# Attention and MLP on one core: weights converted without GpSimd, masks computed from indices, and the MLP's matmuls dealt out singly with a lag

## The chip, the cores and the metric

One core of a Trainium2 chip. The metric is the device time of one launch in microseconds (us), median of repeated runs. The program uses one core, so there is no second core to compare with. The experiments were made on three chips; on each, the kernel before was timed in the same rounds, with medians of 871.7 to 873.1 us.

## The reference, cut to what matters

```python
batch, n_heads, seq, head_dim = (4, 8, 768, 48)          # attention
n_tokens, d_model, d_ff = (3072, 384, 2048)              # MLP

for t in range(S):                                       # gated linear attention with a state
    state = f[:, :, t, :, None] * state + einsum('bhd,bhe->bhde', k[:, :, t], v[:, :, t])
    y[:, :, t] = einsum('bhd,bhde->bhe', q[:, :, t], state)
x = y.transpose(0, 2, 1, 3).reshape(B * S, H * D)        # the bridge
h = x @ w_in                                             # f = sigmoid(f_logit) above
g = h * sigmoid(1.702 * h)
out = g @ w_out
```

`w_in` and `w_out` reach the device as fp64; the kernel has to turn their bits into fp32 itself. Everything else is fp32.

## The kernel before

The attention is cut into 12 units of 256 positions. A unit is a list of parts. A "T" part is four TensorE transposes and a ScalarE copy out of PSUM; a "W" part is a level of scores, which TensorE computes, VectorE scales and masks, and TensorE applies to v. Two units make a pair, whose result xT (turned by DMA) feeds one MLP: 16 blocks "h" of three products of 512 columns, then 64 "o" products of 384 columns. (The trace records two matmuls for each of these products, hence 96 h and 128 o in its lines; "matmul" in the change is one product.) The TensorE order is fixed when the kernel is built, so work for the engine is put between the small dependent steps of the attention by emitting it there.

The conversion of one piece of weights uses three engines:

```python
WI, WO = 256, 192                                        # columns of a piece of w_in, w_out
def load_weights(n, dst, src):
    bits = wp.tile([P, w, 2], I32, tag="bits", bufs=4)
    nc.sync.dma_start(out=bits..., in_=src.bitcast(I32))
    lo, hi = bits[:, :, 0], bits[:, :, 1]
    nc.scalar.activation(sign, hi.bitcast(F32), AF.Sign)
    nc.scalar.activation(a, hi.bitcast(F32), AF.Abs, scale=2.0 ** 112)
    ve.tensor_scalar(a, a, 2.0 ** 97, None, op0=ALU.max)
    ve.tensor_scalar(s.bitcast(I32), a.bitcast(I32), 3, -(1 << 31), ...)      # shift, xor
    ve.tensor_scalar(a.bitcast(I32), s.bitcast(I32), -(1 << 23), None, op0=ALU.bitwise_and)
    ve.scalar_tensor_tensor(a, lo.bitcast(U32), 2.0 ** -52, a, op0=ALU.mult, op1=ALU.mult)
    po.tensor_tensor(a, a, s, ALU.add)                   # GpSimd
    po.tensor_tensor(dst, a, sign, ALU.mult)             # GpSimd
```

The MLP is a list of blocks, and `merge` emits blocks between the parts of a unit (cut):

```python
def mlp_h(g, s, xT, t0, t1):                             # one block: NK = 3 matmuls, sigmoid, product
    ...
    return [lambda ff=ff: block(ff) for ff in range(NFF)]
def mlp_o(g, s):                                         # one block: 4 matmuls
    ...
def merge(parts, fill, share):
    for i, (kind, fn) in enumerate(parts):
        fn()
        at += share(kind, i)
        while done < len(fill) * at / total:
            fill[done](); done += 1
...
for s in range(1, NALL // 2):                            # the schedule: the MLP of pair s in the next two units
    fill = mlp_h(g[s], s, xTs[s], 0, TM) + mlp_o(g[s], s)
    ...
    for j in range(2):
        merge(unit(2 * (s + 1) + j), fill[j * len(fill) // 2:(j + 1) * len(fill) // 2], even)
```

Nearly all DMAs are issued from SyncE's one queue: raw inputs, v, weights, xT and the output. The conversion of the weights is put in as fill too: pieces of `w_in` in unit 0, pieces of `w_out` in units 1 and 2.

## Time and profile before

| | kernel before |
|---|---|
| time, median of 3 runs | 871.22 us (870.77 to 872.17) |
| profiled span | 870.1 us |
| start of unit 1, 2, 3 (first transpose of each on TensorE) | 72.13, 159.94, 206.16 us |
| from the start of unit 3 to the end | 663.9 us |

The last two rows split the kernel into "the start", where the weights are still being converted, and "the rest". The prediction below shows the page and the waits. Here are busy times by stretch, each with the number of instructions. The first line of stretches is unit 0, the second roughly unit 1, the third one pair in the steady part. PEclk is the clock that TensorE was granted, as a share of full speed.

```profile
core 0: us, PE busy (x) PEld busy (x) DVE busy (x) ACT busy (x) POOL busy (x), PEclk, DMA share, GB/s
0.00:72.00 72.00, 29.24 (x592) 23.87 (x592) 50.28 (x105) 24.37 (x56) 41.17 (x65) 0.75 0.79 175
72.00:166.00 94.00, 57.81 (x721) 45.71 (x718) 68.49 (x180) 38.36 (x103) 52.61 (x78) 0.68 0.50 126
335.20:463.70 128.50, 119.57 (x1425) 69.90 (x1424) 43.50 (x61) 30.61 (x50) 6.29 (x12) 0.97 0.30 66
```

At the start no engine is full. In the steady pair TensorE lacks 8.9 us of being full, 6 of them in the one wait for xT that the prediction shows. The other part of those 8.9 us is in small waits, such as these two, where one block of transposes follows another with nothing put between (TensorE's timeline, start and duration; the bracket gives the idle time ahead and what ended it):

```profile
406.92 0.90 PE L199 MATMUL tf<-ident,raw 128*128 128x128 f32 x4
408.50 0.66 PE L199 MATMUL tq<-ident,raw 128*128 128x128 f32 x4 [0.69 <-ACT F L205]
...
411.58 0.60 PE L199 MATMUL tq<-ident,raw 128*128 128x128 f32 x4
412.90 0.66 PE L199 MATMUL tk<-ident,raw 128*128 128x128 f32 x4 [0.73 <-ACT X L207]
```

### The profile page before, as it was taken

Reading aid. Unit: us, or ns where it says so; the run is one execution under the profiler, and the core shown is the slowest. Engines: PE = TensorE matmul, PEld = TensorE weight load, DVE = VectorE, ACT = ScalarE, POOL = GpSimd, SP = SyncE. Lnnn points to the kernel's source line nnn. Section 1 sums busy time; section 2 is a strip of 40 time slices with the busy share of each in tenths; the row PEclk is TensorE's granted clock in tenths of the full one; section 3 lists DMA queues with packets and bytes.
Section 4 is the critical chain, followed back from the end, with each engine's and each line's share of the span. In section 5 each row is a group of like instructions: output and inputs, shape, how many; then the busy total and the mean of one; then the engine's idle time right before and its main releaser. Section 6 shows DMA issues by size and latency. Waiting matters only on the chain.

```text
span 870.1 us, 19829 instructions
## 1 busy us (share of the span) xinstructions
PE 745.9 (86%) x8672; PEld 460.9 (53%) x8672; DVE 345.8 (40%) x611; ACT 223.6 (26%) x429; POOL 126.3 (15%) x204
## 2 busy tenths in 40 slices
PE   2445367899996999996999996999997999989998
PEld 1343355677663555663555663555664555654454
DVE  3787778563330542321452321452322532312200
ACT  2334334433112323112223112223112232111200
POOL 7455555401001001001001001001001001000000
PEclk9855559799998999998999997999999999999999
DMA  9846624514514206223216123117134020000000
GB/s 211 176 117 178 138 75 141 119 27 116 78 58 99 38 11 141 43 73 83 37 29 133 33 85 79 30 39 131 25 90 84 2 84 28 11 26 12 0 19 18
DMA packets 132902, 63.41 MB, mean 73 GB/s; under 512 B 104144, under 2 KB 129744, under 8 KB 132816
## 3 DMA queue, kind: packets, MB, share of 16 engines
q1 hardware_dynamic: 132816, 62.15, 31.1%
q8 instruction: 68, 1.11, 0.6%
q14 instruction: 18, 0.15, 0.1%
HBM read 52.69 MB, written 9.44 MB: 71 GB/s over the span
## 4 chain that ended last, share of the span: by engine, by line
PE 71%; POOL 8%; issue 8%; ACT 4%; DMA 4%; SPq 4%; DVE 1%; POOLq 0%; ACTq 0%; DVEq 0%
PE h L412 28%; PE o L429 27%; PE sc L228 5%; PE y L277 4%; POOL a L140 4%; POOL w_out L141 2%; PE y L382 2%; SPq L394 2%; POOL w_in L141 2%; DMA vn<-v_tok 1%; DMA xT<-yT 1%; ACT X L207 1%; PE tq L199 1%; SPq L167 1%; PE tk L199 1%
## 5 line engine op out<-in xcount | busy, mean ns | idle before, releaser
L412 PE MATMUL h<-xT,w_in 128*128 128x512 f32 (+1 forms) x672 | 282.7, 569 | 31.0 <-DMA xT<-yT 25.7
L429 PE MATMUL o<-w_out,g 128*128 128x384 f32 x768 | 261.9, 491 | 0.0
L412 PEld LDWEIGHTS h<-xT,w_in 128*128 128x128 f32 x672 | 129.8, 202 | 142.1 <-issue 112.8
L429 PEld LDWEIGHTS o<-w_out,g 128*128 128x128 f32 x768 | 141.1, 190 | 90.4 <-issue 2.6
L418 DVE TENSOR_TENSOR g<-h,sg 128x512 f32<-128x512 f32 (+1 forms) x112 | 68.7, 614 | 243.3 <-ACT sg L417 243.3
L417 ACT ACTIVATE sg<-h 128x512 f32<-128x512 f32 (+1 forms) x112 | 59.8, 535 | 203.9 <-PE h L412 202.2
L264 DVE TENSOR_TENSOR X<-X,tot 128x1024 f32<-128x1024 f32 x60 | 73.2, 1220 | 89.9 <-PE sc L228 89.8
L214 POOL TENSOR_TENSOR tot<-F 128x512 f32<-128x512 f32 x12 | 12.7, 1055 | 530.1 <-ACT F L205 464.6
L228 PE MATMUL sc<-X,Kc 48*64 48x64 f32 x1920 | 45.6, 238 | 34.4 <-DVE A L248 34.1
L268 ACT COPY Kc<-X 128x512 f32<-128x512 f32 x60 | 37.7, 628 | 132.9 <-DVE X L264 132.9
L228 PEld LDWEIGHTS sc<-X,Kc 48*64 48x64 f32 x1920 | 37.8, 148 | 61.1 <-issue 27.4
L277 PE MATMUL y<-A,vl 64*48 64x64 f32 (+1 forms) x2688 | 65.4, 243 | 0.0
L248 DVE TENSOR_TENSOR A<-sc,masks 128x512 f32<-128x512 f32 (+1 forms) x84 | 62.9, 759 | 0.0
L277 PEld LDWEIGHTS y<-A,vl 64*48 64x48 f32 x2688 | 55.7, 132 | 2.3 <-issue 2.0
L140 POOL TENSOR_TENSOR a<-a,s 128x192 f32<-128x192 f32 (+1 forms) x56 | 41.1, 734 | 60.5 <-DVE a L139 58.9
L131 ACT ACTIVATE sign<-bits 128x192 f32<-128x192 f32 (+1 forms) x56 | 22.5, 401 | 73.0 <-POOL w_out L141 34.5
L435 ACT COPY osb<-o 128x384 f32<-128x384 f32 x24 | 11.5, 479 | 106.6 <-PE o L429 102.8
L388 ACT COPY yT<-y 48x1024 f32<-48x1024 f32 x24 | 24.2, 1006 | 47.7 <-PE y L382 47.4
L133 DVE TENSOR_SCALAR a<-a 128x192 f32<-128x192 f32 (+1 forms) x56 | 21.6, 387 | 37.1 <-ACT a L132 36.5
L228 PE MATMUL sc<-X 48*64 48x128 f32 (+1 forms) x768 | 27.2, 274 | 9.8 <-DVE A L248 9.1
L218 DVE TENSOR_TENSOR X<-X,F 128x512 f32<-128x512 f32 x24 | 21.3, 886 | 30.9 <-ACT X L207 30.9
L382 PE MATMUL y<-X,st 48*48 48x64 f32 x704 | 25.1, 228 | 9.0 <-DVE st L369 6.9
(38 smaller groups left out, 460.4 us busy)
## 6 DMA issues: line engine op xcount, KB each, us to landing
vl<-v_tok SPq DMA_DIRECT2D x84, 192.0 KB
bits<-in_moe_w_in_dram SPq DMA_DIRECT2D x24, 256.0 KB
bits<-in_moe_w_out_dram SPq DMA_DIRECT2D x32, 192.0 KB
raw<-in_f_logit_dram SPq DMA_DIRECT2D x24, 192.0 KB
raw<-in_q_dram SPq DMA_DIRECT2D x24, 192.0 KB
raw<-in_k_dram SPq DMA_DIRECT2D x24, 192.0 KB
v_tok<-in_v_dram SPq DMA_DIRECT2D x12, 384.0 KB
vn<-v_tok SPq DMA_DIRECT2D x12, 384.0 KB
```

Of the source, the lines that this page charges most:

```text
L140: po.tensor_tensor(a, a, s, ALU.add)
L141: po.tensor_tensor(dst, a, sign, ALU.mult)
L228: nc.tensor.matmul(out[g * HS:(g + 1) * HS, h, a, :], lhsT=lhs(h, a * U + g * G), rhs=rhs(h, a * U + g * G), start=True, stop=True,)
L248: nc.vector.tensor_tensor(A[:, :, c:c + w].rearrange("p h (x t) -> p h x t", t=64), t["sc"][:, :, c:c + w].rearrange("p h (x t) -> p h x t ...
L264: nc.vector.tensor_tensor(qk, qk, by, ALU.mult)
L268: nc.scalar.copy(Kc.rearrange("p (n m) -> p n m", m=m), X[:, 2].rearrange("p (n two m) -> p n two m", two=2, m=m)[:, :, 0, :],)
L277: nc.tensor.matmul(dst(h, g, a), lhsT=t["vl"][g * 64:(g + 1) * 64, u, (2 * a + h) * D:(2 * a + h + 1) * D], rhs=A(h, g, a), start=(start a ...
L382: nc.tensor.matmul(py[rows(h), c // 2, a, c % 2 * C:(c % 2 + 1) * C], lhsT=t["before"][c][rows(h), a], rhs=t["X"][rows(h), 1, x:x + C], st ...
L412: nc.tensor.matmul(ph[:, :T], lhsT=w_in[:, n, ff * P:(ff + 1) * P], rhs=xT[:, n, t0:t1], start=(n == 0), stop=(n == NK - 1),)
L417: nc.scalar.activation(sg[:, :T], ph[:, :T], AF.Sigmoid, scale=1.702)
L418: nc.vector.tensor_tensor(g[ff // FG][:, ff % FG, t0:t1], ph[:, :T], sg[:, :T], ALU.mult)
L429: nc.tensor.matmul(po, lhsT=g[ff // FG][:, ff % FG, tt * P:(tt + 1) * P], rhs=w_out[:, ff, :], start=(ff == 0), stop=(ff == NFF - 1),)
```

## The change

Five things at once. GpSimd and one ScalarE operation leave the conversion, which VectorE then does with six operations (ScalarE keeps one, the Abs); pieces of `w_out` are twice as wide (384 columns), and there are three landing buffers, in which the raw bits arrive, in place of four. The masks come from two index tiles and comparisons. The MLP lags: unit 3 gets 32 of its matmuls fewer, so that half an "o" product is still to do when a pair ends and xT is on its way. And the fill is dealt out matmul by matmul, by columns, where it went by blocks of three or four. At the start, four pieces are emitted ahead of everything, and the rest is spread differently over units 0 to 2.

The diff, cut (cuts marked with `...`):

```diff
-    full = mlp.tile([P, NL, G], F32, tag="g", name="full", bufs=5)
-    nc.gpsimd.memset(full, 1.0)
+    at = [wp.tile([P, 64], I32, tag="bits", name=f"at{j}", bufs=3) for j in range(2)]
+    nc.gpsimd.iota(at[0], ...); nc.gpsimd.iota(at[1], ...)
+    nc.vector.tensor_scalar(at[0], at[0], 63, None, op0=ALU.bitwise_and)
+    nc.vector.tensor_tensor(at[0], at[0], at[1], ALU.bitwise_xor)
     for l, m in enumerate(LEV):
-        ... two nc.gpsimd.affine_select per level, then one nc.gpsimd.tensor_tensor ...
+        nc.vector.tensor_scalar(masks[:, l, :], at[0], float(m), None, op0=ALU.is_lt)
...
-    WI, WO = 256, 192
+    WI, WO = 256, 384
...
-        bits = wp.tile([P, w, 2], I32, tag="bits", name=f"bits_{n}", bufs=4)
+        bits = wp.tile([P, w, 2], I32, tag="bits", name=f"bits_{n}", bufs=3)
...
-        nc.scalar.activation(sign, hi.bitcast(F32), AF.Sign)
         nc.scalar.activation(a, hi.bitcast(F32), AF.Abs, scale=2.0 ** 112)
+        ve.tensor_scalar(si, hi, -(1 << 31), -(1 << 31), op0=ALU.bitwise_and, op1=ALU.bitwise_xor)
         ve.tensor_scalar(a, a, 2.0 ** 97, None, op0=ALU.max)
-        ve.tensor_scalar(s.bitcast(I32), a.bitcast(I32), 3, -(1 << 31), ...)
-        ve.tensor_scalar(a.bitcast(I32), s.bitcast(I32), -(1 << 23), None, op0=ALU.bitwise_and)
+        ve.scalar_tensor_tensor(si, ai, 3, si, op0=ALU.logical_shift_left, op1=ALU.bitwise_xor)
+        ve.tensor_scalar(ai, si, -(1 << 23), None, op0=ALU.bitwise_and)
         ve.scalar_tensor_tensor(a, lo.bitcast(U32), 2.0 ** -52, a, op0=ALU.mult, op1=ALU.mult)
-        po.tensor_tensor(a, a, s, ALU.add)
-        po.tensor_tensor(dst, a, sign, ALU.mult)
+        ve.tensor_tensor(dst, a, s, ALU.add)
...
-        return [lambda ff=ff: block(ff) for ff in range(NFF)]
+        return [(T, lambda ff=ff, n=n: one(ff, n)) for ff in range(NFF) for n in range(NK)]
...
-            while done < len(fill) * at / total:
-                fill[done]()
-                done += 1
+            while fill and done < columns * at / total:
+                w, emit = fill.pop(0)
+                emit()
+                done += w
...
+    LAG = 32 * DM
...
+    for _ in range(4):
+        weights.pop(0)[1]()
+    ...
+    merge(unit(0), weights, W_IN - 4 * WI, windows)
+    first = unit(1)
+    merge(first[:8], weights, W_OUT // 6, steady)
+    fill = both(mlp_h(g[0], 0, 0, U), [weights.pop(0) for _ in range(len(weights) // 2)])
+    merge(first[8:], fill, NFF * NK * U, steady)
+    emit_all(fill)
+    fill = both(mlp_h(g[0], 0, U, TM), weights)
+    merge(unit(2), fill, NFF * NK * U, steady)
+    emit_all(fill)
+    fill = mlp_o(g[0], 0)
     for s in range(1, NALL // 2):
+        fill += mlp_h(g[s], s, 0, TM) + mlp_o(g[s], s)
+    for n in range(3, NALL):
+        merge(unit(n), fill, UNIT - (LAG if n == 3 else 0), steady)
+    emit_all(fill)
```

More of the change, by code (lines that the diff above doesn't have):

```diff
@@ L84 @@
     make_identity(nc, ident)
-    full = mlp.tile([P, NL, G], F32, tag="g", name="full", bufs=5)
-    nc.gpsimd.memset(full, 1.0)
-    for l, m in enumerate(LEV):
-        for base, step, chan in ((0, -m, 1), (m - 1, m, -1)):
-            nc.gpsimd.affine_select(
-                out=full[:, l, :], in_=full[:, l, :], compare_op=ALU.is_ge, fill=0.0, base=base,
-                pattern=[[step, G // m], [0, m]], channel_multiplier=chan,
-            )
-    masks = const.tile([P, NL, 64], F32, name="masks")
-    nc.gpsimd.tensor_tensor(masks, full[:, :, :64], full[:, :, 64:], ALU.add)
+    masks = const.tile([P, NL, 64], F32, name="masks")
+    at = [wp.tile([P, 64], I32, tag="bits", name=f"at{j}", bufs=3) for j in range(2)]
+    nc.gpsimd.iota(at[0], pattern=[[0, 64]], base=0, channel_multiplier=1)
+    nc.gpsimd.iota(at[1], pattern=[[1, 64]], base=0, channel_multiplier=0)
+    nc.vector.tensor_scalar(at[0], at[0], 63, None, op0=ALU.bitwise_and)
+    nc.vector.tensor_tensor(at[0], at[0], at[1], ALU.bitwise_xor)
+    for l, m in enumerate(LEV):
+        nc.vector.tensor_scalar(masks[:, l, :], at[0], float(m), None, op0=ALU.is_lt)
     raw = const.tile([P, 3, NG, H, HS], F32, name="raw")
@@ L118, in load_weights, with tmp @@
             return
-        bits = wp.tile([P, w, 2], I32, tag="bits", name=f"bits_{n}", bufs=4)
+        bits = wp.tile([P, w, 2], I32, tag="bits", name=f"bits_{n}", bufs=3)
         nc.sync.dma_start(out=bits.rearrange("p c two -> p (c two)"), in_=src.bitcast(I32))
         lo, hi = bits[:, :, 0], bits[:, :, 1]
-        def tmp(tag):
-            return wp.tile([P, w], F32, tag=tag, name=f"{tag}_{n}")
-        ve, po = nc.vector, nc.gpsimd
-        sign, a, s = tmp("sign"), tmp("a"), tmp("s")
-        nc.scalar.activation(sign, hi.bitcast(F32), AF.Sign)
+        def tmp(tag, bufs=2):
+            return wp.tile([P, w], F32, tag=tag, name=f"{tag}_{n}", bufs=bufs)
+        ve = nc.vector
+        a, s = tmp("a"), tmp("s")
+        ai, si = a.bitcast(I32), s.bitcast(I32)
         nc.scalar.activation(a, hi.bitcast(F32), AF.Abs, scale=2.0 ** 112)
+        ve.tensor_scalar(si, hi, -(1 << 31), -(1 << 31), op0=ALU.bitwise_and, op1=ALU.bitwise_xor)
         ve.tensor_scalar(a, a, 2.0 ** 97, None, op0=ALU.max)
-        ve.tensor_scalar(
-            s.bitcast(I32), a.bitcast(I32), 3, -(1 << 31), op0=ALU.logical_shift_left, op1=ALU.bitwise_xor
-        )
-        ve.tensor_scalar(a.bitcast(I32), s.bitcast(I32), -(1 << 23), None, op0=ALU.bitwise_and)
+        ve.scalar_tensor_tensor(si, ai, 3, si, op0=ALU.logical_shift_left, op1=ALU.bitwise_xor)
+        ve.tensor_scalar(ai, si, -(1 << 23), None, op0=ALU.bitwise_and)
         ve.scalar_tensor_tensor(a, lo.bitcast(U32), 2.0 ** -52, a, op0=ALU.mult, op1=ALU.mult)
-        po.tensor_tensor(a, a, s, ALU.add)
-        po.tensor_tensor(dst, a, sign, ALU.mult)
+        ve.tensor_tensor(dst, a, s, ALU.add)
     V_HALF = [(1, 0), (1, 1)] + [(m, 0) for m in LEV[1:]]
@@ L403, with mlp_h, one @@
     TM = 2 * U
-    def mlp_h(g, s, xT, t0, t1):
-        def block(ff):
-            if ff % FG == 0 and t0 == 0:
-                g.append(mlp.tile([P, FG, TM], F32, tag="g", name=f"g_{s}_{ff}", bufs=5))
-            T = t1 - t0
-            ph = ps.tile([P, TM], F32, tag="mm", name=f"h_{s}_{ff}_{t0}", bufs=3)
-            for n in range(NK):
-                nc.tensor.matmul(
-                    ph[:, :T], lhsT=w_in[:, n, ff * P:(ff + 1) * P], rhs=xT[:, n, t0:t1],
-                    start=(n == 0), stop=(n == NK - 1),
-                )
-            sg = mlp.tile([P, TM], F32, tag="sg", name=f"sg_{s}_{ff}_{t0}")
-            nc.scalar.activation(sg[:, :T], ph[:, :T], AF.Sigmoid, scale=1.702)
-            nc.vector.tensor_tensor(g[ff // FG][:, ff % FG, t0:t1], ph[:, :T], sg[:, :T], ALU.mult)
-        return [lambda ff=ff: block(ff) for ff in range(NFF)]
+    def mlp_h(g, s, t0, t1):
+        t = {}
+        T = t1 - t0
+        def one(ff, n):
+            if n == 0:
+                if ff % FG == 0 and t0 == 0:
+                    g.append(mlp.tile([P, FG, TM], F32, tag="g", name=f"g_{s}_{ff}", bufs=5))
+                t["ph"] = ps.tile([P, TM], F32, tag="mm", name=f"h_{s}_{ff}_{t0}", bufs=3)
+            ph = t["ph"]
+            nc.tensor.matmul(
+                ph[:, :T], lhsT=w_in[:, n, ff * P:(ff + 1) * P], rhs=xTs[s][:, n, t0:t1],
+                start=(n == 0), stop=(n == NK - 1),
+            )
+            if n == NK - 1:
+                sg = mlp.tile([P, TM], F32, tag="sg", name=f"sg_{s}_{ff}_{t0}")
+                nc.scalar.activation(sg[:, :T], ph[:, :T], AF.Sigmoid, scale=1.702)
+                nc.vector.tensor_tensor(g[ff // FG][:, ff % FG, t0:t1], ph[:, :T], sg[:, :T], ALU.mult)
+        return [(T, lambda ff=ff, n=n: one(ff, n)) for ff in range(NFF) for n in range(NK)]
@@ L421, in mlp_o, with one @@
     def mlp_o(g, s):
         t = {}
-        def some(tt, ff0):
-            if ff0 == 0:
+        def one(tt, ff):
+            if ff == 0:
                 t["po"] = ps.tile([P, DM], F32, tag="mm", name=f"o_{s}_{tt}", bufs=3)
             po = t["po"]
-            for ff in range(ff0, ff0 + 4):
-                nc.tensor.matmul(
-                    po, lhsT=g[ff // FG][:, ff % FG, tt * P:(tt + 1) * P], rhs=w_out[:, ff, :],
-                    start=(ff == 0), stop=(ff == NFF - 1),
-                )
-            if ff0 + 4 == NFF:
+            nc.tensor.matmul(
+                po, lhsT=g[ff // FG][:, ff % FG, tt * P:(tt + 1) * P], rhs=w_out[:, ff, :],
+                start=(ff == 0), stop=(ff == NFF - 1),
+            )
+            if ff == NFF - 1:
@@ L437, in some, with merge, steady, windows @@
                 nc.sync.dma_start(out=out[r0:r0 + P, :], in_=o)
-        return [lambda tt=tt, ff0=ff0: some(tt, ff0) for tt in range(TM // P) for ff0 in range(0, NFF, 4)]
-    def merge(parts, fill, share):
-        total = sum(share(kind, i) for i, (kind, _) in enumerate(parts))
+        return [(DM, lambda tt=tt, ff=ff: one(tt, ff)) for tt in range(TM // P) for ff in range(NFF)]
+    def merge(parts, fill, columns, share):
+        total = sum(share(kind) for kind, _ in parts)
         at = done = 0
-        for i, (kind, fn) in enumerate(parts):
+        for kind, fn in parts:
             fn()
-            at += share(kind, i)
-            while done < len(fill) * at / total:
-                fill[done]()
-                done += 1
-    def even(kind, i):
+            at += share(kind)
+            while fill and done < columns * at / total:
+                w, emit = fill.pop(0)
+                emit()
+                done += w
+    def steady(kind):
         return 3 if kind == "W" else 1
+    def windows(kind):
+        return kind == "W"
     xTs, loads = {}, {}
@@ L473, in load, with both, emit_all @@
         loads[n] = load_v(n)
-    weights = [lambda n=n, p=p: load_weights(n, *p) for n, p in enumerate(pieces_in + pieces_out)]
-    NI = len(pieces_in)
+    weights = [(p[0].shape[1], lambda n=n, p=p: load_weights(n, *p)) for n, p in enumerate(pieces_in + pieces_out)]
+    W_IN, W_OUT = NK * DFF, NFF * DM
+    UNIT = (NFF * NK * TM + TM // P * NFF * DM) // 2
+    LAG = 32 * DM
+    g = {s: [] for s in range(NALL // 2)}
+    def both(one, two):
+        a, b = sum(w for w, _ in one), sum(w for w, _ in two)
+        todo, out, at = list(two), [], 0
+        for w, emit in one:
+            out.append((w, emit))
+            at += w
+            while todo and b - sum(x for x, _ in todo) < b * at / a:
+                out.append((0, todo.pop(0)[1]))
+        return out
+    def emit_all(fill):
+        while fill:
+            fill.pop(0)[1]()
+    for _ in range(4):
+        weights.pop(0)[1]()
     load_raw(0)
     load(0)
-    merge(unit(0), weights[:NI], lambda kind, i: 1)
-    g = {s: [] for s in range(NALL // 2)}
-    u1 = unit(1)
-    merge(u1[:8], weights[NI:NI + 8], lambda kind, i: 1)
-    merge(u1[8:], weights[NI + 8:NI + 16] + mlp_h(g[0], 0, xTs[0], 0, U), lambda kind, i: 1)
-    merge(unit(2), [f for p in zip(mlp_h(g[0], 0, xTs[0], U, TM), weights[NI + 16:]) for f in p], even)
-    merge(unit(3), mlp_o(g[0], 0), even)
-    for s in range(1, NALL // 2):
-        fill = mlp_h(g[s], s, xTs[s], 0, TM) + mlp_o(g[s], s)
-        if s + 1 == NALL // 2:
-            for f in fill:
-                f()
-            continue
-        for j in range(2):
-            merge(unit(2 * (s + 1) + j), fill[j * len(fill) // 2:(j + 1) * len(fill) // 2], even)
+    merge(unit(0), weights, W_IN - 4 * WI, windows)
[8 more added lines that the diff above has]
+    fill = mlp_o(g[0], 0)
+    for s in range(1, NALL // 2):
+        fill += mlp_h(g[s], s, 0, TM) + mlp_o(g[s], s)
+    for n in range(3, NALL):
+        merge(unit(n), fill, UNIT - (LAG if n == 3 else 0), steady)
+    emit_all(fill)
 _INS = ['q', 'k', 'v', 'f_logit', 'moe_w_in', 'moe_w_out']
```

## The prediction

> **What bounds the kernel now.** I read the page first, then the chain of work that ended last, then the timeline of TensorE at the places where that chain leaves TensorE, then the waits of the stretch in which it lies on GpSimd. A "unit" below is the attention of 256 positions of one batch (12 of them); the MLP of a pair of units (the "h" product, then the "o" product) is put between the parts of later units.
>
> The page, part 2: two regimes. For about 165 us TensorE is half idle and at half clock while VectorE and GpSimd are busy (the fp64 weights are converted to fp32 there, 56 pieces); after 205 us TensorE is full with short dips, and the last 88 us are MLP alone.
>
> ```profile
> span 870.1 us, 19829 instructions
> PE   2445367899996999996999996999997999989998
> DVE  3787778563330542321452321452322532312200
> POOL 7455555401001001001001001001001001000000
> PEclk9855559799998999998999997999999999999999
> ```
>
> The chain of work, end of it: one MLP at full clock costs 42.25 + 41.29 = 83.5 us.
>
> ```profile
> 783.03 42.25 PE h L412 x94
> 825.28 41.29 PE o L429 x128
> ```
>
> The dips: TensorE's timeline where a pair of units ends. The last o of the old MLP and a transpose of the next unit are done, then h stands first in TensorE's fixed order and needs xT, which this pair's attention has only just produced and a DMA must turn. The waits of TensorE sum it up.
>
> ```profile
> 395.08 0.60 PE L199 MATMUL tf<-ident,raw 128*128 128x128 f32 x4
> 401.67 2.90 PE L412 MATMUL h<-xT,w_in 128*128 128x512 f32 x3 [5.99 <-DMA xT<-yT]
> ...
> 653.29 0.60 PE L199 MATMUL tf<-ident,raw 128*128 128x128 f32 x4
> 657.10 3.44 PE L412 MATMUL h<-xT,w_in 128*128 128x512 f32 x4 [3.21 <-issue]
> ```
>
> There are five: 7.0 us before 273.2, 6.0 before 401.7, 7.0 before 531.2, 3.2 before 657.1, 3.55 before 781.9, in sum 26.8 us. After each the clock is down: the chain shows the first six h at 5.11, 5.46, 5.46 and 4.32 us where six cost 2.59 later; excess 2.5 + 2.9 + 2.9 + 1.7 = 10.0 us.
>
> The start: in the waits between 83 and 166 us (unit 1) the longest are a ring: ScalarE waits for GpSimd to free the "sign" buffer, VectorE for ScalarE, GpSimd for VectorE; TensorE's scores wait behind it in VectorE's queue.
>
> ```profile
> POOL a L140 <- DVE a L139: 35.1, 28, 3.8
> ACT sign L131 <- POOL w_out L141: 34.5, 24, 3.4
> PE sc L228 <- DVE A L248: 23.5, 5, 6.5
> DVE a L133 <- ACT a L132: 15.3, 17, 2.9
> ```
>
> The reader is to see that no engine is saturated there: pieces go round at (89.3 - 17.0)/23 = 3.14 us for 256 columns and (171.4 - 90.0)/31 = 2.63 us for 192, by the first and last starts of the GpSimd multiplications, while one piece holds GpSimd for 1.2 to 1.5 us. The windows give unit 0 as 0 to 72 us, unit 1 as 72 to 166, unit 2 as 166 to 206.
>
> **What the Trainium skill says.** "GPSIMD Engine Reference", section Performance versus the Vector engine: two-input elementwise work is about half as fast there. The trace agrees: an addition of 128x256 takes 741 ns on GpSimd, VectorE's product of 128x256 420 ns. The same page, section Key points: it shares SBUF interfaces with VectorE, with contention when VectorE runs in a two-port mode. The trace agrees: the 256-wide TENSOR_SCALAR takes 0.29 us when GpSimd is idle (13.3 us), and 0.70 us at 15.9 us beside a GpSimd addition. "VectorE: DVE Perf Modes", section on the perf-mode tiers: fp32 tensor_scalar runs at 2x, tensor_tensor at 1x; here 0.29 against 0.42 us at 256 columns. "TensorE: Matmul & The Clock Gate", Part 1: the clock halves after an idle window of about 3.4 us and needs as much work to return; PEclk 0.50 between 40 and 80 us, and the slow h above, agree.
>
> **The change, part by part.**
>
> *Masks.* Fourteen GpSimd operations (8.2 us, until 9.5 us) become two iotas and eight VectorE operations of 64 columns. GpSimd's next work is at 14.5 us, so this was hidden: about 0.
>
> *Conversion.* Removed per piece: one ScalarE operation and two of GpSimd. VectorE goes from three TENSOR_SCALAR and one two-input operation to three and three. In the timeline independent TENSOR_SCALARs start 0.20 us apart (31.30, 31.51, 31.71) and a two-input one holds the engine 0.33 at 256 columns; at 192 it is 0.17 and 0.27. So 3 x 0.20 + 3 x 0.33 = 1.6 us, with some waits on the operation before 1.75 us for 256 columns; extended to 384 (0.26 and 0.45), 2.13, say 2.35 us. 24 x 1.75 + 16 x 2.35 = 80 us of VectorE. Attention costs VectorE per unit 6 x 1.14 + 1.14 + 6 x 0.60 + 2 x 0.60 + 7 x 0.39 = 15.5 us, the gating of half an h 16 x 0.33 = 5.3 us. So VectorE is what bounds units 0 and 1:
> - Unit 0: first weights land at 12.5 us as before, 19 pieces come ahead of its state update in VectorE's order: 12.9 + 19 x 1.75 + 15.5 = 62; with three landing buffers instead of four some waits on DMA: 68 us (was 72). Little gain, since VectorE takes over what GpSimd did.
> - Unit 1: 5 x 1.75 + 9 x 2.35 + 15.5 + 5.3 = 51, plus the tail of state and y and the thin transposes at its start: 57 us (was 94). Half the pieces at a lower cost per column, and no ring: this is the largest single gain.
> - Unit 2: 7 x 2.35 + 15.5 + 5.3 = 37 on VectorE, under TensorE's 21 (half of h) + 18 (attention, below). Its first h needs unit 1's xT; about 10 us passed from the last y to the h at 531.2, and only 3.6 us of other matmuls stand between, so 4 to 6 us of waiting: 45 us (was 40).
> Sum: 170 us instead of 206.
>
> *Lag.* Unit 3 gets 32 of 64 o matmuls, and everything later is 32 x 0.645 = 20.6 us behind, so at a pair's end half an o product is still to do while xT travels (10 us). TensorE's order confirms it: h of the second MLP stands in the middle of unit 4. All five gaps and slow clocks go: 26.8 + 10.0 = 36.8 us. The tail grows from 83.5 to 104 us, but that is work taken from the middle: no cost in the sum.
>
> *Dealing.* One pair takes 401.67 to 531.22 = 129.55 us; less 83.5, 7.0 and 2.9 that is 36.1, or 18.05 us for each attention with its bubbles. Two transposes ran with nothing between where a block was not due (0.7 us each; 2.8 us a pair in the waits). Even dealing takes perhaps 0.5 us a unit over eight units: 4 us. Unit 3, with half its fill (1.9 us a part where score, scaling and masking need about 2.0; 0.65 us between transposes that need 1.2), loses 4 us. Together 0.
>
> Sum: 170 + 41.3 + 5 x 83.5 + 9 x 18.05 + 3.5 (last copy and store, 866.6 to 870.1) = 795 us of span; with the unrounded gaps before, 870.1 - 36 - 37 = 797. The timed median is 1.1 us above the span: **798 us**.
>
> **The rivals.**
> First, VectorE as the new bound, worse than I take it: the sign operation reads every second word, and if it and the waits between dependent steps (0.32 instead of 0.20 us in the trace) apply throughout, a piece costs 2.3 and 3.1 us: (0.55 x 24 + 0.75 x 16) = 25 us more, unit 0 ending at 78. For it: VectorE is already 8 tenths busy from 20 to 60 us. Against: the built order interleaves two pieces nearly everywhere, and part of the present busy time is contention with GpSimd that ends. It would make 820 us.
> Second, DMA: three landing buffers; if a piece's refill (issue to usable, about 4 us at the start) paces the ring, 3 pieces per 6 us, 2.0 us each, close to VectorE's rate; for 384 columns 2.7. It costs some 8 us more, mostly in unit 0: 806 us.
> Third, the lag gains nothing because the gaps only move: xT comes late from a queue of issues (ten of 0.6 us each), and now stalls the h in mid-unit. Against it: 30 us of matmuls stand ahead of that h. It would make 835 us.
> Fourth, better than thought: with TensorE at full clock from unit 0's end and VectorE fully used (137 us for three units, from 12.9), unit 2 ends at 158: 785 us.
>
> **Range and chances.** The lag's 37 us are nearly certain, for the order is fixed and the slack is threefold. The start may be anything from 156 to 186 us. So 798 us, 8 in 10 between 783 and 816. Faster by over 2% needs under 853.8: 0.97; within 2% 0.02; slower 0.01.
>
> **What would show it.** Right: no TensorE wait of h on xT after 210 us, but one of 4 to 6 us near 130; h groups of six at 2.6 us from unit 3 on; unit 3 about 43 us, later units 59 to 60; VectorE at 9 tenths to about 125 us; conversions of w_in ending near 75 us; GpSimd under 5%. Wrong: VectorE with idle time on DMA or ScalarE before the sign step (DMA rival); pieces at more than 2.2 and 3 us of VectorE (first rival); unit 1 longer than 70 us; new TensorE waits between score and mask in units 4 to 11, which would mean that finer dealing exposed the attention's own chain.

## The result, and the profile after

The changed kernel is correct. Its time is 798.37 us (796.19 to 798.55, 4 runs), that of the kernel before in the same rounds 871.69 us (870.77 to 872.42, 4 runs). The ratio is 0.915, with a 95% interval from 0.9135 to 0.9172. (A ratio here is the mean time of one kernel's runs over that of the other's runs of the same rounds, so it is not quite the ratio of the medians.) So the forecast of 798 us was met within 0.4 us. The stages say that this is less good than it looks:

| | before | predicted | after |
|---|---|---|---|
| unit 0 | 72.1 | 68 | 67.9 |
| unit 1 | 87.8 | 57 | 69.9 |
| unit 2 | 46.2 | 45 | 50.65 |
| start of unit 3 | 206.2 | 170 | 188.45 |
| unit 3 | 59.5, then a gap of 7.0 | 43 | 39.1 |
| a later unit | 64.7 | 59 to 60 | 57.7 |
| from the start of unit 3 to the end | 663.9 | 625 to 627 | 607.9 |

The units are taken from the first transpose of each on TensorE, so the "before" row for unit 1 differs from the rougher boundaries (72 and 166 us) that the prediction took from the page. A later unit is (718.22 - 265.64)/7 before and (631.61 - 227.55)/7 after, from the starts of units 4 and 11. The start came out 18.5 us worse than forecast and the rest 17 to 19 us better. Two errors cancelled.

The page of the changed kernel, parts 1 and 2:

```profile
span 796.3 us, 19489 instructions
PE 722.1 (91%) x8672; PEld 447.8 (56%) x8672; DVE 339.0 (43%) x635; ACT 204.4 (26%) x357; POOL 39.5 (5%) x80
PE   3525498699999999999999999999999999999998
DVE  4695898763524435313445233444134353102200
POOL 2001000101010010010010010010010000000000
PEclk9997589899999999999999999999999999999999
```

A slice is 20 us. From 160 us on TensorE is at 9 without the dips of before, and its clock stays up. GpSimd has gone from 126.3 to 39.5 us. VectorE is at 9 from 40 to 60 us and at 8 or 9 from 80 to 140, but falls to 5 from 60 to 80, where TensorE is at 5 too: something else held both there.

Busy time by stretch, with the columns as before: unit 0, unit 1, unit 2, and one steady pair.

```profile
0.00:68.00 68.00, 28.29 (x593) 22.89 (x594) 49.90 (x147) 16.95 (x34) 4.50 (x14) 1.00 0.76 165
68.00:138.00 70.00, 48.70 (x706) 39.09 (x707) 56.23 (x138) 24.62 (x49) 3.48 (x6) 0.71 0.64 164
138.40:188.50 50.10, 41.35 (x702) 33.56 (x702) 32.30 (x65) 16.58 (x34) 3.24 (x6) 0.90 0.37 84
343.30:458.50 115.20, 115.20 (x1425) 68.06 (x1424) 43.01 (x61) 30.54 (x50) 6.86 (x12) 1.00 0.36 73
```

The last line is the clearest result: TensorE is busy 115.20 of 115.20 us, for the same 1425 matmuls that took 128.50 us before. The second line is the disappointment: VectorE is busy 56.2 of 70 us, so it leaves 13.8 idle in the unit that it was supposed to bound.

The largest piece of that idle time is one wait. SyncE's queue, then VectorE's timeline:

```profile
63.13 5.17 SPq L163 DMA_DIRECT2D vl<-v_tok  x7
68.39 0.42 SPq L167 DMA_DIRECT2D vn<-v_tok  x1
68.92 1.43 SPq L118 DMA_DIRECT2D bits<-in_moe_w_in_dram  x3
```

```profile
76.01 0.29 DVE L131 TENSOR_SCALAR s<-bits 128x256 int32<-128x256 int32 x1 [8.00 <-DMA bits<-in_moe_w_in_dram]
```

Three pieces of weights stand behind eight loads of v in one queue. The first load of v could not go before the old v was used; the queue's own waits say for how long:

```profile
SPq L163 <- PE y L273: 3.3, 1, 3.3
```

So the queue stands still for 3.3 us, then issues v for 5.6 us (5.17 + 0.42), then the weights, which need 7.09 us to land (from 68.92 to the sign operation at 76.01). VectorE's last reads of the three buffers had ended at 62.0, 63.4 and 66.0 us, so two of the three pieces could have been asked for more than 5 us earlier. VectorE runs out of other work at 68 and waits 8.0 us.

The end of a pair, where the kernel before had a gap of 6 or 7 us (TensorE's timeline near 373 us): the h that begins the next MLP follows the last o without any wait.

```profile
371.84 1.56 PE L429 MATMUL o<-w_out,g 128*128 128x384 f32 x4
373.24 2.74 PE L412 MATMUL h<-xT,w_in 128*128 128x512 f32 x6
```

The transposes of the next unit, which answer to the two waits of before at 408.50 and 412.90: one or two h products (two or four records) now stand between every two of them, and none waits.

```profile
402.80 0.60 PE L195 MATMUL tf<-ident,raw 128*128 128x128 f32 x4
403.23 1.02 PE L412 MATMUL h<-xT,w_in 128*128 128x512 f32 x2
404.10 0.65 PE L195 MATMUL tq<-ident,raw 128*128 128x128 f32 x4
404.58 1.88 PE L412 MATMUL h<-xT,w_in 128*128 128x512 f32 x4
406.30 0.60 PE L195 MATMUL tq<-ident,raw 128*128 128x128 f32 x4
406.74 1.02 PE L412 MATMUL h<-xT,w_in 128*128 128x512 f32 x2
```

Of TensorE's waits after 190 us, two are left in the whole list:

```profile
PE sc L224 <- DVE A L244: 0.5, 1, 0.5
PE tf L195 <- ACT F L201: 0.3, 1, 0.3
```

### The profile page after: what moved, and what is told of

Its sections match the earlier page's. It is cut to its first block, busy times and chain, and to the rows that moved or that the text cites. A ratio compares the mean times of both kernels' runs of the same rounds, so it can differ in the third digit from the quotient of the medians.

```text
span 796.3 us, 19489 instructions
## 1 busy us (share of the span) xinstructions
PE 722.1 (91%) x8672; PEld 447.8 (56%) x8672; DVE 339.0 (43%) x635; ACT 204.4 (26%) x357; POOL 39.5 (5%) x80
## 4 chain that ended last, share of the span: by engine, by line
PE 82%; DVE 9%; DMA 4%; ACT 1%; issue 1%; SPq 1%; POOL 0%; DVEq 0%; ACTq 0%; POOLq 0%
PE o L429 32%; PE h L412 29%; PE sc L224 7%; PE y L273 5%; DMA bits<-in_moe_w_in_dram 3%; PE y L378 2%; DVE X L260 2%; PE tk L195 2%; PE tkn L331 1%; PE sc L347 1%; PE tq L195 1%; DVE s L133 1%; DVE a L136 1%; PE tf L195 1%; DVE A L244 1%
## 5 line engine op out<-in xcount | busy, mean ns | idle before, releaser
L412 PE MATMUL h<-xT,w_in 128*128 128x512 f32 (+1 forms) x672 | 273.1, 548 | 6.6 <-DMA xT<-yT 6.4
L429 PE MATMUL o<-w_out,g 128*128 128x384 f32 x768 | 265.8, 492 | 0.0
L429 PEld LDWEIGHTS o<-w_out,g 128*128 128x128 f32 x768 | 139.5, 190 | 86.0 <-issue 4.5
L412 PEld LDWEIGHTS h<-xT,w_in 128*128 128x128 f32 x672 | 124.0, 195 | 100.4 <-issue 82.6
L273 PE MATMUL y<-A,vl 64*48 64x64 f32 (+1 forms) x2688 | 64.7, 241 | 0.0
L384 ACT COPY yT<-y 48x1024 f32<-48x1024 f32 x24 | 24.1, 1006 | 59.4 <-PE y L378 50.9
L224 PE MATMUL sc<-X 48*64 48x128 f32 (+1 forms) x768 | 24.9, 272 | 12.0 <-DVE A L244 12.0
L224 PEld LDWEIGHTS sc<-X 48*64 48x64 f32 x768 | 19.9, 148 | 25.7 <-issue 24.7
L362 DVE TENSOR_TENSOR st<-st,tot 128x192 f32<-128x192 f32 x44 | 15.7, 357 | 41.4 <-POOL tot L210 40.1
L130 ACT ACTIVATE a<-bits 128x256 f32<-128x256 f32 (+1 forms) x40 | 19.2, 486 | 51.3 <-DMA bits<-in_moe_w_in_dram 24.3
L195 PE MATMUL tq<-ident,raw 128*128 128x128 f32 x96 | 17.3, 310 | 12.2 <-ACT F L201 10.7
L365 DVE TENSOR_TENSOR st<-st,sc 128x192 f32<-128x192 f32 x44 | 15.5, 353 | 25.2 <-PE sc L347 24.1
```

The lines of the kernel that those rows point to most:

```text
L195: nc.tensor.transpose(pt[:, a, g, :], raw[:, j, g, 2 * (a0 + a):2 * (a0 + a + 1), :].rearrange("p h d -> p (h d)"), ident)
L224: nc.tensor.matmul(out[g * HS:(g + 1) * HS, h, a, :], lhsT=lhs(h, a * U + g * G), rhs=rhs(h, a * U + g * G), start=True, stop=True,)
L273: nc.tensor.matmul(dst(h, g, a), lhsT=t["vl"][g * 64:(g + 1) * 64, u, (2 * a + h) * D:(2 * a + h + 1) * D], rhs=A(h, g, a), start=(start a ...
L384: nc.scalar.copy(yT[rows(h)].rearrange("p a g t -> p g a t"), py[rows(h)])
L412: nc.tensor.matmul(ph[:, :T], lhsT=w_in[:, n, ff * P:(ff + 1) * P], rhs=xTs[s][:, n, t0:t1], start=(n == 0), stop=(n == NK - 1),)
L429: nc.tensor.matmul(po, lhsT=g[ff // FG][:, ff % FG, tt * P:(tt + 1) * P], rhs=w_out[:, ff, :], start=(ff == 0), stop=(ff == NFF - 1),)
```

## The experiments

All start from the changed kernel unless said otherwise; "start" is the time at which unit 3 begins, "the rest" is from there to the end of the profiled span. For the changed kernel they are 188.45 and 607.9 us.

### What the lag alone is worth: `no_lag`

```diff
-    LAG = 32 * DM
+    LAG = 0
```

> The changed kernel with the lag set to 0, all else as changed. My sizes from the trace of the kernel before (five gaps of 26.8 us in sum, 10.0 us of slow clock after them) make this 798 + 37 = 835 us, and the trace should show TensorE's first h of each later pair waiting 3 to 7 us for xT, five times. A rival: finer dealing alone already closes part of the gaps, because the attention of a pair's last unit now ends earlier beside its own matmuls; then 815 us or less.

Measured: 828.76 us (826.91 to 831.68), 30.4 more than the changed kernel. The start is the same (188.06); the rest is 640.2, so 32.3 us longer. TensorE's waits after 190 us are the old gaps:

```profile
PE h L412 <- DMA xT<-yT: 22.4, 4, 7.9
PE h L412 <- issue: 1.9, 1, 1.9
```

These are 24.3 us of waits; the other 8 of the 32.3 follow them: after four of the gaps the first four h records take 3.47 to 3.75 us, where four take 1.88 a little later, so some 1.7 us a gap (the prediction put the slow clock after the gaps at 10). The lag does what it was said to do, but is worth 30 to 32 us and not 37. The result lies between the two theories, nearer to the first.

### What dealing by single matmuls is worth: `blocks`

```diff
+    def blocks(one, n):          # joins n neighbouring entries of the fill into one, emitted together
+        ...
-    fill = both(mlp_h(g[0], 0, 0, U), [weights.pop(0) ...])
+    fill = both(blocks(mlp_h(g[0], 0, 0, U), NK), [weights.pop(0) ...])
...
-        fill += mlp_h(g[s], s, 0, TM) + mlp_o(g[s], s)
+        fill += blocks(mlp_h(g[s], s, 0, TM), NK) + blocks(mlp_o(g[s], s), 4)
```

> The changed kernel with the lag, but the MLP dealt out in whole blocks of 3 h or 4 o matmuls as before. If dealing is worth what the prediction gave it (4 us, given back in unit 3), this is within 4 us of the changed kernel, 798 to 802 us. If it is worth the 2.1 us a unit that the two traces differ by after gaps and clock are taken off (16.3 against 18.4 us for the attention of a unit), this is 798 + 9 x 2.1 = 817 us, with TensorE idle at transposes that follow one another.

Measured: 819.45 us (818.44 to 819.84), 21.1 more. The start is no worse (187.23); the rest is 630.9, 23.0 more. The waits of TensorE after 190 us, and its timeline in one unit:

```profile
PE tq L195 <- ACT F L201: 6.4, 9, 0.7
PE tk L195 <- ACT X L203: 6.3, 9, 0.7
PE sc L224 <- DVE A L244: 1.6, 1, 1.6
PE y L273 <- issue: 1.1, 1, 1.1
PE tkn L331 <- DVE X L260: 1.0, 1, 1.0
PE tq L195 <- ACT X L203: 0.7, 1, 0.7
```

```profile
355.27 0.60 PE L195 MATMUL tf<-ident,raw 128*128 128x128 f32 x4
356.56 0.66 PE L195 MATMUL tq<-ident,raw 128*128 128x128 f32 x4 [0.69 <-ACT F L201]
```

One transpose block to the next is 1.29 us here (355.27 to 356.56). In the changed kernel a block takes 0.43 us of TensorE's order (402.80 to 403.23) before its h begin. So an uncovered pair costs about 0.86 us, though the wait in brackets is only 0.69: the rest is presumably the last matmuls running out alone, where otherwise the next would have begun. Waits in the list add up to 17.1 us against 0.8 with single matmuls; with (0.86 - 0.69) us for each of 18 pairs, 3 us more, that is 19 of the 23 us measured. The other 4 are not traced.

The two experiments and the two kernels make a square for the rest: 663.9 (neither, the kernel before), 640.2 (dealing only), 630.9 (lag only), 607.9 (both). Each part is worth nearly the same with and without the other: the lag 32.3 or 33.0, dealing 23.0 or 23.7. The corner "neither" is the kernel before itself, not a build of the new one.

### The start, conversion or order: `after_gpsimd` and `before_dve`

`after_gpsimd` puts the old conversion into the changed kernel, with its widths and four landing buffers. `before_dve` puts the new conversion, with three buffers, into the kernel before, at 192 columns for `w_out`.

```diff
# after_gpsimd
-    WI, WO = 256, 384
+    WI, WO = 256, 192
-    def load_weights(...):   # six VectorE operations, bufs=3
+    def load_weights(...):   # as in the kernel before, bufs=4
# before_dve, from the kernel before
-    def load_weights(...):   # Sign and Abs on ScalarE, four VectorE, two GpSimd operations
+    def load_weights(...):   # Abs on ScalarE, six VectorE operations, bufs=3
```

> The changed kernel with the old conversion (two GpSimd operations and two of ScalarE a piece, w_out in 192 columns, four landing buffers); the order of the start, lag, dealing and masks as changed. If conversion on VectorE is worth the 36 us of the prediction, 834 us; if it is worth only what the start shrank in the traces (206.2 to 188.5), 816 us. Steady part as changed (607 us from unit 3 on).

> The kernel before with only the conversion changed (six VectorE operations, none of GpSimd, one of ScalarE; three landing buffers), in the old order with 192 columns of w_out a piece. The prediction's reason (a ring of three engines at 3.14 and 2.63 us a piece is replaced by VectorE at 1.75) would shrink the start by 30 us or more: 840 us or less. If the conversion is worth what it is worth inside the changed kernel (807.6 against 798.4), it is 9 us: 861 to 863 us. If the order of the start and the conversion only work together, less than 5 us: 867 us or more.

Measured: `after_gpsimd` 807.60 us (806.55 to 808.65), start at 198.9. `before_dve` 860.24 us (857.80 to 862.92), ratio to the kernel before 0.986 (0.9833 to 0.9892), start at 194.4. The start by both: 206.2 (neither), 194.4 (new conversion only), 198.9 (new order only), 188.45 (both). So the new conversion is worth 10.5 to 11.8 us, and the new order of the start 6.0 to 7.3. This square is not exact: "new order" takes in the new masks and the single dealing, and the wide pieces of `w_out` go with the conversion in `after_gpsimd` but are left out of `before_dve`. Neither the width nor the number of landing buffers was tried alone. The old conversion's ring is still there in the new order, in the waits from 84 to 150 us:

```profile
POOL a L138 <- DVE a L137: 31.7, 22, 5.4
ACT sign L129 <- POOL w_out L139: 25.8, 17, 3.8
```

Removing the ring was called "the largest single gain", with most of 36 us. It is worth about 11.

### Whether VectorE bounds the start: `light_dve`

Four of the six VectorE operations of a piece are taken out. The result is wrong (relative error 5.5), with the scale changed so that it stays finite. By the distances between starts that is 2 x 0.20 + 2 x 0.33 us for each of 24 pieces and 2 x 0.27 + 2 x 0.465 for each of 16 wide ones, 49 us of VectorE.

```diff
-        ve.tensor_scalar(a, a, 2.0 ** 97, None, op0=ALU.max)
-        ve.scalar_tensor_tensor(si, ai, 3, si, op0=ALU.logical_shift_left, op1=ALU.bitwise_xor)
-        ve.tensor_scalar(ai, si, -(1 << 23), None, op0=ALU.bitwise_and)
-        ve.scalar_tensor_tensor(a, lo.bitcast(U32), 2.0 ** -52, a, op0=ALU.mult, op1=ALU.mult)
+        # scale of the Abs: 0.01
```

> The changed kernel with only the first and the last of the six VectorE operations of a piece left (a wrong result on purpose; same transfers, same ScalarE work, same order). If VectorE's occupation is what bounds the start, as predicted, up to 24 x 1.07 + 16 x 1.45 = 49 us of VectorE go and the start shrinks by 20 us or more: 778 us or less. If the start hangs on the order and landing of transfers (weights behind the v transfers in one queue, 8 us of VectorE idle at 76 us), it shrinks by under 10 us: 788 to 796 us.

Measured: 774.27 us (773.91 to 774.93), 24.1 less; the start is at 164.2. Half of the 49 us shows in the time, so VectorE does bound the start, in part: unit 0 is 13.7 us shorter, unit 1 8.9, unit 2 1.7. Unit 1 still takes 61.0 us, and in it VectorE waits 8.9 us for weights, about as much as in the changed kernel (8.0), though it is far less busy:

```profile
DVE s L131 <- DMA bits<-in_moe_w_in_dram: 8.9, 1, 8.9
```

### The queue that weights are issued from: `bits_gpsimd` and `bits_act`

```diff
-        nc.sync.dma_start(out=bits..., in_=src.bitcast(I32))
+        nc.gpsimd.dma_start(out=bits..., in_=src.bitcast(I32))     # bits_act: nc.scalar
```

> The changed kernel with the weights' transfers issued from GpSimd instead of the common queue. In the changed kernel VectorE waits 8.0 us for a piece at 68 to 76 us, which was issued behind seven v transfers that waited for TensorE. If that place in the queue is the cause and the wait sets the end of unit 1, 6 to 8 us less: 790 to 792 us. If the wait comes from the transfers' own traffic, or is hidden, 796 to 800 us.[...]

> The same from ScalarE's queue. As the GpSimd form if ScalarE's queue never blocks, 790 to 792 us; but an issue that waits for a landing buffer now holds back ScalarE's attention copies behind it, which may cost more than it gains: 800 to 815 us.

Measured: from GpSimd 787.59 us (786.97 to 789.55), 10.8 less; units 0 to 2 end at 65.7, 133.1 and 177.3. From ScalarE 792.92 us (790.99 to 793.99), 5.5 less; 66.8, 133.1 and 184.3. VectorE's waits of `bits_gpsimd` from 40 to 140 us have no wait of 8 us any more:

```profile
DVE g L419 <- ACT sg L418: 4.4, 5, 2.5
DVE s L131 <- DMA bits<-in_moe_w_in_dram: 4.1, 2, 2.2
```

The transfers and buffers are the same. From GpSimd the kind of queue differs too (the page counts these transfers as software_dynamic, those of SyncE and ScalarE as hardware_dynamic), but from ScalarE the kind is the same, and there too the wait of 8 us is gone (VectorE's longest wait for weights is 3.3 us). That shows that the wait of 8.0 us came mainly from the place in SyncE's queue. It does not show that unit 1 was 8 us too long for it. Against the changed kernel, `bits_gpsimd` gains 2.2 us in unit 0, 2.5 in unit 1 and 6.5 in unit 2. With the wait gone, unit 1 still takes 67.4 us, and VectorE is busy 59.05 of them (columns as before):

```profile
65.70:133.10 67.40, 50.05 (x707) 39.69 (x706) 59.05 (x144) 25.11 (x49) 12.85 (x23) 0.73 0.69 176
```

A likely reason that GpSimd's queue does better than ScalarE's is that GpSimd has less else to do (39.5 us busy in the changed kernel, ScalarE 204.4); that was not tested. GpSimd's queue also helps unit 2: the h that needs unit 1's xT waits 2.77 us there, against 6.37 in the changed kernel and 9.63 with ScalarE's queue.

### The wait for xT in unit 2: `hold`

The lag's idea, applied at the start: 24 h matmuls of unit 1 are kept for unit 2, where xT is on its way.

```diff
-    merge(first[8:], fill, NFF * NK * U, steady)
-    emit_all(fill)
-    fill = both(mlp_h(g[0], 0, U, TM), weights)
-    merge(unit(2), fill, NFF * NK * U, steady)
+    HOLD = 24 * U
+    merge(first[8:], fill, NFF * NK * U - HOLD, steady)
+    fill += both(mlp_h(g[0], 0, U, TM), weights)
+    merge(unit(2), fill, NFF * NK * U + HOLD, steady)
```

> The changed kernel with 24 of the 48 h matmuls of the first half held back into unit 2, so that the first h on the new half of xT comes some 12 us later in TensorE's order. The 6.4 us wait at 138 to 145 us and the slow clock after it should go and the start shrink by 5 to 7 us: 791 to 793 us. If unit 2 then waits on VectorE (the remaining weights) instead, under 2 us.

Measured: 792.79 us (791.85 to 793.86), 5.6 less; the start is at 183.0. The wait of h in unit 2, 6.37 us in the changed kernel as shown here, is gone.

```profile
144.77 2.20 PE L412 MATMUL h<-xT,w_in 128*128 128x256 f32 x4 [6.37 <-DMA xT<-yT]
```

### A theory that fell: `early`

Unit 1 looked like two stretches one after the other: the first waits for weights, the second, from 102 to 138 us, has TensorE at 34.3 of 36.2 us. If the second were TensorE's, beginning the h earlier would shorten unit 1.

```diff
-    merge(first[:8], weights, W_OUT // 6, steady)
+    merge(first[:6], weights, W_OUT // 6, steady)
-    merge(first[8:], fill, ...)
+    merge(first[6:], fill, ...)
```

> The changed kernel with the first h product (and the w_out pieces dealt with it) beginning two parts earlier in unit 1, at its first score instead of its third. My theory of the failed step: unit 1 is two stretches one after the other, a first one of 34 us in which TensorE is busy 15 us at half clock because no MLP matmul may stand there yet, and a second one of 36 us full of TensorE work; VectorE's total does not add up over both. Then h moved into the first stretch shortens the second: unit 1 shrinks by 3 to 7 us and the whole to 791 to 795 us. If VectorE's occupation bounds the unit as a whole, as the prediction had it, nothing changes: 797 to 800 us.

Measured: 798.51 us (797.19 to 799.02), the same as the changed kernel; the start is at 188.3. The theory fell. The stretch after the wait for weights in `early`, columns as before, shows whose it is: VectorE is busy 49.7 of 52.0 us.

```profile
84.00:136.00 52.00, 42.12 (x687) 34.17 (x686) 49.69 (x123) 18.43 (x39) 0.00 (x0) 0.93 0.63 158
```

TensorE had more to do early and waited for VectorE all the same.

### All together: `all_three`

Weights issued from GpSimd, the h of unit 1 from part 6 on, and 16 h matmuls held for unit 2 (the three diffs above, with `HOLD = 16 * U`).

> The changed kernel with the weights' transfers issued from GpSimd, the h product of unit 1 begun two parts earlier, and 16 of its matmuls held back into unit 2. Singly the first gave 10.8 us and holding back gave 5.6 us. If the three waits are separate, the start ends near 172 us and the kernel takes 779 to 783 us; if VectorE takes over as the bound once the waits are gone, 784 to 788 us, no better than the first alone.

Measured: 784.27 us (783.33 to 784.48), ratio to the kernel before 0.899 (0.8969 to 0.9008); the start is at 174.6. It beats both kernels, but only 3.3 us better than `bits_gpsimd` alone.

### The masks: `after_oldmasks` and `own_indices`

`after_oldmasks` is the changed kernel with the fourteen GpSimd operations of before for its masks.

```diff
-    at = [wp.tile([P, 64], I32, tag="bits", ...) for j in range(2)]
-    nc.gpsimd.iota(...); nc.gpsimd.iota(...); ... eight VectorE operations ...
+    full = mlp.tile([P, NL, G], F32, tag="g", name="full", bufs=5)
+    ... memset, affine_select, tensor_tensor on GpSimd ...
```

> The changed kernel with the old masks (14 GpSimd operations until about 9.5 us). GpSimd's next work starts at about 14 us, so nothing waits for it: within 1 us of the changed kernel, 797.5 to 799.5 us. If the landing buffers that the new masks' indices occupy at the start matter, the old masks are a little faster, 796 us.

Measured: 795.83 us (794.45 to 796.13), about 2.5 less than the changed kernel; its start is at 186.3. So the new masks seem to cost a little; this is 0.3%, and the intervals of the two ratios to the kernel before overlap (0.9099 to 0.9141 against 0.9135 to 0.9172). The first operations of the conversion on VectorE, in `after_oldmasks` and in the changed kernel:

```profile
3.80 1.95 DVE L133 TENSOR_SCALAR s<-bits 128x256 int32<-128x256 int32 x2 [2.06 <-DMA bits<-in_moe_w_in_dram]
```

```profile
12.51 0.29 DVE L131 TENSOR_SCALAR s<-bits 128x256 int32<-128x256 int32 x1 [9.71 <-DMA bits<-in_moe_w_in_dram]
```

With the old masks the weights' first transfers stand ahead of the raw inputs and land 8.7 us earlier. A possible reason is that the two index tiles take two of the three buffers named "bits". `own_indices` tries it, on top of `all_three`:

```diff
-    at = [wp.tile([P, 64], I32, tag="bits", name=f"at{j}", bufs=3) for j in range(2)]
+    at = [wp.tile([P, 64], I32, tag=f"at{j}", name=f"at{j}", bufs=1) for j in range(2)]
```

> The form with all three edits of the start (784.3 us), and the two index tiles of the new masks in buffers of their own instead of in two of the weights' landing buffers. With the old masks, which do not take those buffers, the changed kernel was 2.5 us faster, because the first weights then came ahead and VectorE began at 3.8 instead of 12.5 us. If the taken buffers are the cause, 780.5 to 782.5 us and VectorE's first conversion before 10 us. If the gain came from something else in the old masks' order, 784 us within 1.

Measured: 783.63 us (782.99 to 784.95), start at 175.4. That is 0.6 less than `all_three`, within the scatter of both. It can't decide: with the weights issued from GpSimd, the first of them went out at 1.54 us and VectorE began on them at 6.77 us in `all_three` already (1.53 and 6.59 us here). Why the old masks let the first weights go sooner stays open. `own_indices` has the lowest median of all correct kernels run, 0.898 (0.8964 to 0.8994) of the kernel before, but not shown to be better than `all_three`.

## Why the prediction was right or wrong

The total was right by luck: two opposite errors of 17 to 19 us met. By its own steps:

*Bound of the kernel before: right.* The start was bound by a ring of engines and not by one; the later dips were h waiting for xT. `no_lag` brings those waits back at the same kind of place (24.3 us against 26.8). Only "half clock" for about 165 us is too broad: by windows of 20 us, the granted clock was 0.50 to 0.59 from 40 to 120 us and 0.81 or more before and after. Nor do the slow h all agree with the idle window of 3.4 us that it took from the skill: in `no_lag` the clock was 0.54 from 620.8 to 624.5 us, right after an idle time of 1.93 us.

*Masks, "about 0": perhaps slightly wrong.* They seem to cost about 2.5 us, and the trace differs at the very first transfers. The prediction looked only at when GpSimd was next needed.

*Conversion, cost of a piece: right.* The operations start 0.20 and 0.33 us apart at 256 columns, 0.27 and 0.47 at 384, so a piece costs 1.6 or 2.2 us. The first rival (2.3 and 3.1 us) fell: the sign operation, which reads every second word, takes 0.29 us like the others.

*Unit 0, "68 us": right (67.9).*

*Unit 1, "57 us": failed.* It took 69.9. The sum had two holes. VectorE was busy 56.2 us instead of 51: 12 wide pieces ran there and not 9, for the built order lets three of unit 2's pieces go ahead in VectorE's queue (3 x 2.2 = 6.6 us). And it was idle 13.8 us where about 6 were allowed for, 8.0 of them in the one wait for weights behind the loads of v. The wait is worth less than its length: with it gone, unit 1 still takes 67.4 us from GpSimd's queue and 66.3 from ScalarE's, and ends 4.7 us earlier in both; in the first of them VectorE is busy 59.05 us. `early` says the same, and in the changed kernel itself VectorE is busy 48.5 of the 54.0 us from 84 us on. So the step that failed is VectorE's load in unit 1, and behind it the wait; how the 12.9 us divide between the two is not settled. The second rival named the right kind of wait, "DMA", but as a slow refill of three buffers spread over unit 0; it was the place in the queue, at one moment of unit 1, and changing the queue takes it away. The sign that the prediction asked for ("VectorE with idle time on DMA … before the sign step") is there. So is the late end of the `w_in` conversions, 90.7 us where "near 75" was expected.

*Unit 2, "45 us": low by 5.7.* The wait for xT came as said, 6.37 us where "4 to 6" was expected, at 138 us instead of 130. Another 2.1 us went to scores waiting for VectorE. TensorE's busy time was 41.4 where 39 was reckoned, at a clock of 0.90. `hold`, which puts other matmuls ahead of that h, gains 5.6 us.

*"Sum: 170 us instead of 206": failed by 18.5,* 13 of them in unit 1 and 5.7 in unit 2.

The fourth rival (785 us, with TensorE at full clock from the end of unit 0) did not happen: the granted clock was 0.71 in unit 1.

*Lag, "26.8 + 10.0 = 36.8 us": right in mechanism, oversized.* The marginal worth is 32 to 33 us in the rest, 30.4 in time. All five gaps went, and the third rival (the gaps only move) fell.

*Dealing, "Even dealing takes perhaps 0.5 us a unit …", "Together 0": failed.* It is worth 23 us in the rest (21.1 in time). Two terms were mis-sized. The visible waits of the kernel before were 2.8 us a pair, 1.4 a unit, as the prediction itself says, but all of them went, not just a part; with the time in which the last matmuls run out alone it is about 0.86 us for each of two uncovered pairs a unit, and the remaining scattered waits add some 0.4 a unit. And unit 3 did not lose 4 us for its thinner fill: it took 39.1 us, not 43.

*The rest together:* 36.8 + 0 was predicted against 56.0 measured, and `no_lag` and `blocks` split that as 32.3 + 23.0.

## What to carry to other kernels

Check a right total stage by stage: here two wrong terms cancelled to 0.4 us. Fill between small dependent steps is worth dealing in the smallest units that the order allows, and an uncovered step costs more than the wait that is printed for it (0.86 against 0.69 us here). Before an engine is called the bound of a stretch, look at what stands ahead of its inputs in their queue, for here an unrelated load that had to wait held the weights behind it. But a wait's length is not its worth: 8.0 us were taken away and unit 1 became 2.5 us shorter, with VectorE busy 59 of the 67.4 us left.

## What the Trainium skill lacked or had wrong

- "DMA: Bandwidth & Descriptors", section Issuing engines are not separate DMA queues, says that issuing from several engines "will only save the time on the sequencer it takes to initiate the DMA". Here more than such time was saved: the loads of v took 5.6 us of SyncE's queue to issue, but the first of them also waited 3.3 us at its head for a matmul; weights whose buffers were being freed stood behind, and VectorE was idle for 8.0 us. Moving the weights to GpSimd's queue won 10.8 us, to ScalarE's 5.5. That section does not mention what a wait in the issuing queue does to the transfers behind it.
- "VectorE: DVE Perf Modes", the perf-mode tier table, has no row for `scalar_tensor_tensor`: with two tensor inputs, in fp32 at 256 columns, it takes 0.41 to 0.42 us, like `tensor_tensor`.
- No page that I looked up sizes an uncovered dependent step on TensorE: 0.86 us for a block of four transposes that waits for ScalarE to read the block before, of which 0.69 is shown as a wait.
